# Another recording order for the 586 steps of a fused scan and GELU MLP, with 33 of them on other engines

## The chip, the cores and the metric

The kernel runs on one core of one Trainium2 chip. The metric is the device time in microseconds (us) of one execution; the time of a kernel is the median of its runs. One execution is also recorded by the hardware profiler, and all lines of profiles and traces in this document come from such an execution.

## The reference

A chunked linear recurrence is followed by a two-layer MLP. For each of 4 batches and 8 heads (768 positions, head dimension 32, state size 16):

```python
cum  = np.cumsum(log_a_chunk);  L = exp(cum_i - cum_j) * causal
y    = ((C @ B.T) * L) @ x  +  (C @ state) * exp(cum)          # per chunk
state = exp(sum(log_a_chunk)) * state + sum_j B_j x_j * exp(cum_end - cum_j)
# heads are laid side by side: 3072 tokens x 256
h = tokens @ w_in            # 256 -> 2048
g = gelu_tanh(h)
out = g @ w_out              # 2048 -> 256, 3072 x 256, float32
```

The inputs are float32; the kernel multiplies in bf16 and accumulates in float32.

## The kernel before

**Tiling.** Chunks of 128 positions are used, 6 to a batch, 24 in all. Two chunks make a *unit* u of 256 tokens; there are 12 units, three to a batch. A name such as `s1.3.5` is one step: kind, unit, index.

**The steps of a unit.** `load_x.u` brings x and `castx.u` (L593) casts it to bf16. `G.u` (L599) makes the products of C and B of four head pairs into two PSUM banks ga and gb; `M.u.0` and `M.u.1` (L612, DVE) multiply them by the causal mask. `D.u` (L629) makes the state updates of the two chunks into a bank of the pool hp; `S` (L677) and `SP` (L689), both on DVE, carry the state from chunk to chunk and spread it for the next product. `Y.u` (L642) sums both parts of the output of the scan into the bank yb, and `yev.u` (L673) copies that, as bf16, to where the MLP reads it. Then come eight first products `s1.u.0` to `s1.u.7` (L708: four matmuls of 128x256 into one hp bank), each followed by `gelu.u.i` (L720, ACT), which reads the bank and frees it, and eight second products `s2.c.q` (L725: four matmuls; four q to a chunk c, all into the one bank o, near the end into yb too). `oev.c` (L739) copies the bank o to SBUF, and `store.c` (L744) sends it out. For u from 4 to 11, `G.u` and `D.u` are recorded as a part of `Y.u-1`.

**The steps of a batch.** B and C of a batch are loaded by `load_bc` (L164) and scaled by decay factors: `mul.b.0` (B) and `mul.b.1` (C) (L479). For batch 1 they are turned by TensorE (`T.1.i`, L490, six transposes into ga or gb), copied out (`E.1.i`, L512), C is masked into two halves (`F.1`, L519, two DVE instructions), and B is turned once more (`N.1`, L526, into ga; `bn.1`, L532, copies it out, so that G.3 may write ga again). For batches 2 and 3 a round trip through DRAM does this (`load_wr`, `load_tr`, `load_bn`). The last two chunks of batch 0 have steps of their own of the same kind: `mul1.i` (L442), `T1.i` (L448), `bh1` (L465), `ce1.i` (L458), `N1` (L468), `bn1` (L475). Their factors come from a scan `R` (L375) by the DVE transposes `tp2` (L378, four), `tp6.q` (L385, four) and the reciprocals `recip1` and `recip.1.4` (L382, L389); `pe` and `pp` (L393, L400) make the decay of a whole chunk.

**Weights.** `load_wi.q` and `load_wo.q` bring a quarter of a weight each; `wi.q.k` and `wo.q.k` (L329, L332) cast halves of it to bf16.

**What sets the order.** Every engine runs its instructions in the order in which they were recorded, and the semaphores follow from what reads and writes which tile. The order is a string, `ORDERED` (L17 to L70), of step names; a loop at L945 calls them one after another. `name:A`, `:D` or `:P` moves a step to ACT, DVE or POOL, other than its default. `~n` records n blocks of 128 columns of matmuls on zeros, and `s1.1.3+10` puts ten such blocks ahead of that step; they keep TensorE busy and compute nothing (L705). Buffers that order the work: hp has two banks (each s1, each D), o has one, ga, gb and yb one each, output tiles six.

```python
    for w in ORDERED.split():
        ...
            w, _, n = w.partition("+")
            name, _, e = w.partition(":")
            s = steps[name]
            s.eng, s.pre = e or s.eng, int(n or 0)
            s.fn()
```

Of the kernel before, what the change touches and what calls it, by code (L numbers as in the profile page):

```python
# [19 lines left out]
ew.1.1:A mulc.1 c_bmask c_m8 tw.2 mulb ~4 tw.0 peq ew.0.2:A clip ew.0.1 load_wi.1 ew.0.0:A ew.1.2  # L20
# [6 lines left out]
wo.0.1 T1.0 s1.1.1 T1.1 gelu.1.0 bh1 N1 gelu.1.1 s1.1.2 tp6.0 s1.1.3+10 bn1 ce1.1 load_wo.2
castx.2.None SP.3 wo.0.0 ce1.0 gelu.1.2 gelu.1.3 G.2 s1.1.4 recip.1.4 s1.1.5 gelu.1.4 M.2.1
mul.1.1:P s2.0.0.0.o D.2 M.2.0 load_x.4 gelu.1.5 s2.0.1.0.o s1.1.6 T.1.1 gelu.1.6 S.2.0 s1.1.7
SP.4 Y.2 mul.1.0 yev.2.0.2:D gelu.1.7 wo.1.0 wo.1.1 T.1.0 E.1.1:A castx.3.None:A s1.2.0 wo.2.0  # L30
s1.2.1 E.1.0 wo.2.1 load_wo.3 load_bc.2.1 N.1 gelu.2.0 F.1 s1.2.2 bn.1:D G.3 gelu.2.1 gelu.2.2 D.3
s1.2.3 s2.0.0.1.o S.3.0 S.3.1 load_bc.2.0 gelu.2.3 s1.2.4 M.3.1 s2.0.1.1.o s1.2.5 SP.6 gelu.2.4
s1.2.6 M.3.0 gelu.2.5 wo.3.0:D gelu.2.6 s2.0.0.2.o castx.4.None s1.2.7 Y.3 gelu.2.7 wo.3.1:D
s2.0.1.2.o S.4.0 yev.3.0.2 S.4.1 s2.0.0.3.o oev.0 load_x.5 s1.3.0 s1.3.1 mul.2.1 s2.0.1.3.o
load_wr.2.1 load_x.6 gelu.3.0 gelu.3.1 s1.3.2 oev.1:D SP.8 s1.3.3 s2.1.0.0.o gelu.3.2 M.4.0
gelu.3.3 SP.7 s2.1.0.1.o s2.1.0.2.o s2.1.0.3.o oev.2:D s1.3.4 s1.3.5 s2.1.1.0.o gelu.3.4 M.4.1
mul.2.0:P castx.5.None:A s2.1.1.1.o Y.4 S.5.0 s2.1.1.2.o load_wr.2.0 s2.1.1.3.o load_tr.2.1
load_bn.2 oev.3:D gelu.3.5 s1.3.6 s1.3.7 s2.2.0.0.o yev.4.0.2 load_tr.2.0 gelu.3.6 s1.4.0 SP.9
M.5.1 gelu.3.7 s2.2.0.1.o store.0 store.2 gelu.4.0 s1.4.1 castx.6.None:A s1.4.2 SP.10 s2.2.0.2.o
load_x.7 s2.2.0.3.o gelu.4.1 oev.4:D gelu.4.2 s1.4.3 s1.4.4 load_bc.3.1 s2.2.1.0.o s2.2.1.1.o  # L40
s2.2.1.2.o gelu.4.3 gelu.4.4 s2.2.1.3.o s1.4.5 oev.5 s1.4.6 gelu.4.5 M.5.0 s2.3.0.0.o F.2 store.1
Y.5 s2.3.0.1.o s2.3.0.2.o yev.5.0.2 gelu.4.6 s2.3.0.3.o s1.4.7 S.6.0 gelu.4.7 load_bc.3.0 S.6.1
store.3 s1.5.0 oev.6:D SP.12 s2.3.1.0.o gelu.5.0 s1.5.1 s2.3.1.1.o gelu.5.1 castx.7.None:A
mul.3.1:P s2.3.1.2.o s1.5.2 gelu.5.2 M.6.1 s2.3.1.3.o s1.5.3 M.6.0 Y.6 oev.7:D S.7.0 gelu.5.3
load_x.8 s1.5.4 S.7.1 s2.4.0.0.o s2.4.0.1.o s1.5.5 SP.13 gelu.5.4 load_wr.3.1 yev.6.0.2
castx.8.None store.4 load_x.9 gelu.5.5 SP.14 s2.4.0.2.o s2.4.0.3.o oev.8 s1.5.6 s1.5.7 mul.3.0
castx.9.None s2.4.1.0.o gelu.5.6 load_wr.3.0 gelu.5.7 M.7.0 s2.4.1.1.o s1.6.0 M.7.1 load_tr.3.1
Y.7 S.8.0 load_tr.3.0 gelu.6.0 s1.6.1 s1.6.2 s2.4.1.2.o gelu.6.1 yev.7.0.2:D gelu.6.2 s2.4.1.3.o
oev.9:D M.8.0 s1.6.3 gelu.6.3 SP.16 s1.6.4 s2.5.0.0.o s1.6.5 gelu.6.4 gelu.6.5 M.8.1 SP.15
s2.5.0.1.o s1.6.6 load_bn.3 s2.5.0.2.o s1.6.7 gelu.6.6 s2.5.0.3.o s1.7.0 oev.10:D gelu.6.7 s1.7.1  # L50
gelu.7.0 s2.5.1.0.o s1.7.2 store.5 gelu.7.1 s2.5.1.1.o gelu.7.2 s1.7.3 gelu.7.3 s1.7.4 gelu.7.4
store.9 F.3 s2.5.1.2.o s1.7.5 s1.7.6 gelu.7.5 s2.5.1.3.o s1.7.7 gelu.7.6 store.6 Y.8 oev.11
yev.8.0.2:D gelu.7.7 S.9.0 load_x.10 s2.6.0.0.o s2.6.0.1.o s2.6.0.2.o S.9.1 s1.8.0 gelu.8.0
s2.6.0.3.o s1.8.1 gelu.8.1 oev.12:D s1.8.2 gelu.8.2 s2.6.1.0.o castx.10.None:D store.10 store.11
store.7 s1.8.3 gelu.8.3 s2.6.1.1.o s1.8.4 gelu.8.4 s1.8.5 s2.6.1.2.o s2.6.1.3.o SP.18 M.9.1
gelu.8.5 s1.8.6 M.9.0 store.8 oev.13 gelu.8.6 Y.9 store.12 s2.7.0.0.o s2.7.0.1.o S.10.0 s2.7.0.2.o
yev.9.0.2:D s2.7.0.3.o S.10.1 s1.8.7 oev.14 s1.9.0 load_x.11 castx.11.None:A gelu.8.7 M.10.0
s2.7.1.0.o s2.7.1.1.o SP.21 s1.9.1 s2.7.1.2.o s2.7.1.3.o gelu.9.0 SP.20 gelu.9.1 oev.15 s1.9.2
M.10.1 SP.19 gelu.9.2 Y.10 s1.9.3 gelu.9.3 store.15 S.11.0 s1.9.4 M.11.0 s2.8.0.0.o s1.9.5
gelu.9.4 store.14 s2.8.0.1.o gelu.9.5 s2.8.0.2.o SP.22 s2.8.0.3.o s1.9.6 store.13 gelu.9.6  # L60
oev.16:D s1.9.7 gelu.9.7 yev.10.0.2:D s2.8.1.0.o s1.10.0 s2.8.1.1.o s1.10.1 gelu.10.0 s1.10.2
s2.8.1.2.o gelu.10.1 s1.10.3 s2.8.1.3.o M.11.1 oev.17:D gelu.10.2 s1.10.4 store.17 gelu.10.3
s1.10.5 Y.11 yev.11.0.2:D gelu.10.4 s2.9.0.0.o s1.10.6 gelu.10.5 s2.10.0.0.yb s2.9.0.1.o
s2.10.0.1.yb s1.10.7 s2.10.0.2.yb s2.9.0.2.o gelu.10.6 s2.9.0.3.o s1.11.0 gelu.10.7 s1.11.1 oev.18
s2.9.1.0.o gelu.11.0 store.16 s2.10.0.3.yb s1.11.2 s2.9.1.1.o oev.20 gelu.11.1 s2.9.1.2.o
gelu.11.2 s1.11.3 s2.9.1.3.o gelu.11.3 oev.19:D s1.11.4 s1.11.5 s2.11.0.0.yb gelu.11.4 s1.11.6
gelu.11.5 s2.10.1.0.o store.20 s1.11.7 gelu.11.6 s2.11.0.1.yb s2.10.1.1.o s2.10.1.2.o store.19
s2.10.1.3.o gelu.11.7 oev.21:D s2.11.0.2.yb s2.11.0.3.yb s2.11.1.0.o oev.22:D s2.11.1.1.o store.22
# [915 lines left out]
```

## Time and profile before

| | us |
|---|---|
| median of 3 runs (118.0, 118.29, 121.6) | 118.29 |
| span of the profiled execution, first to last instruction | 116.9 |
| what lies around the span, against the median | 1.4 |
| TensorE matmuls busy in the span | 110.1 |
| DVE busy | 69.4 |
| ACT busy | 72.1 |
| POOL busy | 21.4 |

The profile gives no time of the profiled execution other than its span. A line of the timeline has the start, the time from the first start to the last end, engine, source line, operation, tiles, shapes and count; in square brackets stands how long the engine was idle before it and what it waited for. `PE` is TensorE, `SPq` the DMA queue that SyncE issues to. Where a line has a count over 1 its instructions follow each other.

### The profile page before, as it was taken

To read this page: it belongs to the slowest core of one execution; us is meant where nothing else is said; L and a number is where in the kernel's file an instruction comes from. 1 tells how busy PE (TensorE), PEld (TensorE's weight loads), DVE (VectorE), ACT (ScalarE), POOL (GpSimd) and SP (SyncE) were. 2 spreads that over 40 slices of the span, in tenths; PEclk is the share of its full clock that TensorE was granted. 3 is DMA by queue.
4 is the path that set the end of the run, shared out by engine and by line. 5 is a ranking of instruction groups with operands and counts; after the bars stand their busy time and mean duration, and the time that the engine had idled before them with its cause. 6 is when DMAs were issued, how large, how long until landed. Compare 5 with 4: busy or idle time off the path is not lost.

```text
span 116.9 us, 3379 instructions
## 1 busy us (share of the span) xinstructions
PE 110.1 (94%) x1426; PEld 92.0 (79%) x1426; DVE 69.4 (59%) x140; ACT 72.1 (62%) x139; POOL 21.4 (18%) x38
## 2 busy tenths in 40 slices
...
PEclk9999999999999999999999999999999999999999
...
GB/s 26 228 332 357 281 252 178 208 288 257 305 143 90 185 47 219 213 253 200 72 25 171 121 163 63 0 140 98 40 6 63 71 0 52 43 0 50 45 47 132
DMA packets 43007, 15.97 MB, mean 137 GB/s; under 512 B 36657, under 2 KB 41457, under 8 KB 42993
## 3 DMA queue, kind: packets, MB, share of 16 engines
...
q8 instruction: 11, 0.18, 0.6%
q10 hardware_dynamic: 192, 0.13, 0.5%
...
HBM read 11.04 MB, written 3.93 MB: 128 GB/s over the span
## 4 chain that ended last, share of the span: by engine, by line
PE 75%; DMA 8%; DVE 6%; SPq 6%; issue 2%; POOL 1%; ACT 0%; DVEq 0%; POOLq 0%
PE o_ps L735 33%; PE hp L717 30%; DMA bcf<-in_B_dram 8%; PE yb L735 3%; SPq L190 3%; PE ga L603 3%; PE yb L658 2%; DVE m L613 2%; PE yb L667 2%; DVE ce L523 1%; SPq L150 1%; DVE bh L327 1%; DVE bc L484 1%; SPq L159 1%; SPq L183 1%
## 5 line engine op out<-in xcount | busy, mean ns | idle before, releaser
L721 ACT ACTIVATE gT<-hp 128x512 bf16<-128x512 f32 x96 | 54.3, 596 | 25.0 <-PE hp L717 24.6
L717 PE MATMUL hp<-xm,w_in_sb 128*128 128x256 bf16 x384 | 53.3, 273 | 0.6 <-ACT gT L721 0.4
L735 PE MATMUL o_ps<-w_out_sb,gT 128*128 128x256 bf16 x352 | 47.3, 273 | 0.0
L717 PEld LDWEIGHTS <-w_in_sb 128*128 128x128 bf16 x384 | 41.4, 114 | 3.5 <-issue 1.9
L735 PEld LDWEIGHTS <-gT 128*128 128x128 bf16 x384 | 37.0, 98 | 4.9 <-issue 1.1
L327 DVE COPY o_sb<-o_ps 128x256 f32<-128x256 f32 x13 | 5.5, 425 | 23.8 <-PE o_ps L735 20.4
L613 DVE TENSOR_TENSOR m<-ga,tri 128x1024 bf16<-128x1024 f32 x12 | 14.6, 1218 | 0.1
L613 DVE TENSOR_TENSOR m<-gb,tri 128x1024 bf16<-128x1024 f32 x11 | 13.4, 1219 | 0.7 <-PE gb L603 0.7
L323 ACT ACTIVATE o_sb<-o_ps 128x256 f32<-128x256 f32 x9 | 3.5, 385 | 9.2 <-PE o_ps L735 9.2
L705 PE MATMUL yb<-wz 128*128 128x512 bf16 (+3 forms) x23 | 7.6, 481 | 1.1 <-DVE wz L220 1.1
L691 DVE SCALAR_TENSOR_TENSOR sp_new<-s_new,pend,bmask 128x256 bf16<-128x256 f32 x17 | 7.9, 476 | 0.0
L327 DVE CAST xm<-yb 128x512 bf16<-128x512 f32 x6 | 4.1, 687 | 5.8 <-PE hp L636 4.8
L684 DVE SCALAR_TENSOR_TENSOR s_new<-s_new,pend,hp 128x64 f32<-128x64 f32 x13 | 3.6, 279 | 6.4 <-PE hp L636 6.2
L705 PEld LDWEIGHTS <-wz 128*128 128x128 bf16 x26 | 3.0, 120 | 5.1 <-issue 3.2
L667 PE MATMUL yb<-m,x 128*32 128x128 bf16 x192 | 6.1, 220 | 0.0
L603 PE MATMUL ga<-ce,bh 32*128 32x256 bf16 x48 | 4.7, 273 | 1.3 <-DVE bn L327 0.9
L484 POOL TENSOR_TENSOR bc<-bc_t,pt 128x768 bf16<-128x768 f32 x2 | 3.0, 1494 | 13.8 <-DMA bc_t<-in_C_dram 13.7
L658 PE MATMUL yb<-ce,sp_new 128*32 128x128 bf16 x160 | 5.3, 221 | 0.0
L603 PE MATMUL gb<-ce,bh 32*128 32x256 bf16 x48 | 4.7, 273 | 0.0
L735 PE MATMUL yb<-w_out_sb,gT 128*128 128x256 bf16 x32 | 4.6, 273 | 0.0
L667 PEld LDWEIGHTS <-x 128*32 128x32 bf16 x192 | 3.8, 97 | 0.8 <-issue 0.8
L323 ACT ACTIVATE xm<-yb 128x512 bf16<-128x512 f32 x6 | 3.6, 595 | 1.1 <-PE hp L636 1.1
...
## 6 DMA issues: line engine op xcount, KB each, us to landing
...
```

Source lines behind the costliest of these rows:

```text
L323: nc.scalar.activation(o, i, AF.Copy)
L327: nc.vector.tensor_copy(out=o, in_=i)
L484: (nc.gpsimd if eng == "POOL" else nc.vector).tensor_tensor(out=d["bc16"][:, i], in0=d["bc"].rearrange("p i h (r n) -> p i r h n", r=R6)[: ...
L603: nc.tensor.matmul(out=gbank(g)[:, 256 * k:256 * k + 256], lhsT=bh_of(2 * u + k)[gs], rhs=ce_of(2 * u + k)[gs], start=True, stop=True, til ...
L613: nc.vector.tensor_tensor(out=m_of(u)[:, 2 * i:2 * i + 2].rearrange("p g k e t -> p (g k e) t"), in0=gx[i].rearrange("p g (k t) -> p (g k) ...
L658: nc.tensor.matmul(out=y4[32 * j:32 * j + 32, k, w], lhsT=sp[:, 32 * h:32 * h + 32], rhs=ce_of(gc)[:, h % 2], start=first(j), stop=False, ...
L667: nc.tensor.matmul(out=y4[32 * j:32 * j + 32, k, w], lhsT=X16[u][:, k, 32 * h:32 * h + 32], rhs=m[:, h // 2, h % 2, :], start=first(j), st ...
L691: nc.vector.scalar_tensor_tensor(out=sp_new.rearrange("p (g d) -> p g d", g=4), in0=(XN[0][:, H * D:H * D + 64] if gc == 0 else state[("s" ...
L705: nc.tensor.matmul(out=t[:, 0:m * 128], lhsT=wz, rhs=w3.to_broadcast([128, m, 128]), start=True, stop=True, skip_group_check=True)
L717: nc.tensor.matmul(out=hp[:, j * T:(j + 1) * T], lhsT=w_in_k[:, w, q, k], rhs=xm[:, w, u * T:(u + 1) * T], start=(w == 0), stop=(w == 1))
L721: nc.scalar.activation(gts[u][:, 2 * i:2 * i + 2], hps.pop((u, i)).rearrange("p (j t) -> p j t", j=2), AF.Gelu_apprx_tanh)
L735: nc.tensor.matmul(out=ops[gc], lhsT=gts[u][:, fi, k * Q:(k + 1) * Q], rhs=w_out_sb[:, fi, :], start=(fi == 0 and (u > 0 or k == 0)), stop ...
```

## The change

Only the string `ORDERED` is changed. It names the same 586 steps. As the recorded instruction lists of the two kernels stand:

- Up to `s1.0.0` every engine's order is the same; `c_wz` is written ahead of the loads, but it is the first DVE instruction in both.
- All DMAs on SyncE's queue stand in the same order, loads, round trips and stores.
- After `s1.0.0`, TensorE, DVE, ACT and POOL each have another order.
- The ten blocks of zeros at `s1.1.3` are gone.
- 33 steps change engine: to DVE `ce1.0`, `ce1.1`, `E.1.1`, `mul.1.1`, `wo.1.1`, `castx.6`, `oev` 0, 8, 11, 13, 15; to POOL `wi.3.0`, `mul.1.0`, `castx.3`, `wo.3.0`, `mul.2.1`, `castx.5`, `castx.11`; to ACT `yev` 2, 7, 8, 9, 10, 11, `bn.1`, `wo.2.1`, `wo.3.1`, `castx.10`, `oev` 2, 6, 7, 12, 22. Among them `mul.1.0` and `mul.1.1` swap DVE and POOL.

The stretch in question, by engine, up to G.3:

```
before PE:   s1.0.0 G.1 s1.0.1..6 Y.1 pp s1.0.7 s1.1.0 T1.0 s1.1.1 T1.1 N1 s1.1.2 (10 blocks) s1.1.3 G.2 s1.1.4 s1.1.5
             s2.0.0.0 D.2 s2.0.1.0 s1.1.6 T.1.1 s1.1.7 Y.2 T.1.0 s1.2.0 s1.2.1 N.1 s1.2.2 G.3 D.3
after PE:    s1.0.0 G.1 s1.0.1..6 Y.1 pp T1.0 T1.1 s1.0.7 N1 s1.1.0 s1.1.1 G.2 D.2 s1.1.2 s1.1.3 s2.0.0.0 s1.1.4 s2.0.1.0
             s1.1.5 s1.1.6 Y.2 T.1.0 s1.1.7 s1.2.0 T.1.1 N.1 s1.2.1 s1.2.2 s2.0.0.1 s2.0.1.1 D.3 G.3
before DVE:  SP.1 M.1.1 M.1.0 wi.3.0 SP.2 pe tp6.2 tp2 tp6.3 recip1 S.1.1 tp6.1 tp6.0 SP.3 recip.1.4 M.2.1 M.2.0 S.2.0
             SP.4 mul.1.0 yev.2 E.1.0 F.1 bn.1
after DVE:   tp2 recip1 M.1.0 SP.1 SP.2 M.1.1 pe tp6.0 S.1.1 tp6.2 tp6.3 tp6.1 ce1.1 ce1.0 recip.1.4 S.2.0 M.2.1 M.2.0
             SP.4 SP.3 mul.1.1 E.1.0 wo.1.1 E.1.1 F.1
before POOL: ... wi.3.1 mul1.0 mul1.1 wo.0.1 castx.2 wo.0.0 mul.1.1 wo.1.0 wo.1.1 wo.2.0 wo.2.1 castx.4 mul.2.0 mul.3.1
after POOL:  ... wi.3.1 wi.3.0 mul1.1 mul1.0 wo.0.1 castx.2 wo.0.0 mul.1.0 castx.3 wo.1.0 wo.2.0 wo.3.0 castx.4 mul.2.1 castx.5 mul.2.0 mul.3.1
```

The diff, cut to its first lines; the rest of the string is changed in the same manner:

```diff
-load_aq.0 load_aq.1 load_aq.2 load_aq.3 c_wz load_bc0.1 c_ident c_m4 c_sel c_tri c_zero load_bc0.0
+c_wz load_aq.0 load_aq.1 load_aq.2 load_aq.3 load_bc0.1 c_ident c_m4 c_sel c_tri c_zero load_bc0.0
...
-load_wi.3 S.1.0 s1.0.0 SP.1 xn.2 load_bc1.1 wi.2.0 gelu.0.0 G.1 s1.0.1 s1.0.2 M.1.1 M.1.0
-load_bc1.0 load_wo.0 wi.3.0:D gelu.0.1 wi.2.1 s1.0.3 load_x.2 SP.2 pe wi.3.1 gelu.0.2 load_bc.1.1
+S.1.0 s1.0.0 xn.2 tp2 gelu.0.0 G.1 wi.2.0 s1.0.1 xn.3 recip1 M.1.0 s1.0.2 wi.2.1 gelu.0.1 s1.0.3
+load_bc1.1 SP.1 SP.2 M.1.1 pe tp6.0 gelu.0.2 s1.0.4 wi.3.1 wi.3.0 S.1.1 tp6.2 mul1.1:P gelu.0.3
...
```

From Y.3 on, both orders weave s1 of a later unit with s2 of an earlier one. The new one starts the second products of a unit earlier: `s2.1.0.0` follows Y.3 at once, where before seven steps of s2 and s1 of other chunks stood between.

More of the change, by code (lines that the diff above doesn't have):

```diff
@@ L17 @@
 ORDERED = """
[L18 removed]
+c_wz load_aq.0 load_aq.1 load_aq.2 load_aq.3 load_bc0.1 c_ident c_m4 c_sel c_tri c_zero load_bc0.0
 c_unp load_a.0:A clipq load_x4 Rq tpq recip0 c_cz mulc.0 ~59 tw.1 load_wi.0 c_warm load_a.1:A
[L20 removed]
+ew.1.1:A mulc.1 c_bmask c_m8 tw.2 mulb ~4 tw.0 peq ew.0.2 clip ew.0.1 load_wi.1 ew.0.0:A ew.1.2
@@ L27 @@
[L27 to L68, printed above, removed]
```

49 lines of the change are left out of this document (45 added, 4 removed).

## The prediction

> **What bounds the kernel now.** I read the page first, then the busy time by stretch, then the waits of TensorE with its timeline, and last the timelines of the engines that it waited for. The page:
>
> ```profile
> span 116.9 us, 3379 instructions
> PE 110.1 (94%) x1426; PEld 92.0 (79%) x1426; DVE 69.4 (59%) x140; ACT 72.1 (62%) x139; POOL 21.4 (18%) x38
> ...
> PEclk9999999999999999999999999999999999999999
> ```
>
> TensorE is busy for 94% of the span, at the full granted clock. Where the other 6% lies is told by three stretches, cut at the first s1 (12.50), at G.3 (29.69) and at the end of TensorE's work (columns: length, then busy time and instructions of each engine):
>
> ```profile
> 12.50:29.69 17.19, 15.34 (x197) 11.66 (x198) 15.99 (x30) 14.58 (x30) 9.55 (x15) 1.00 1.04 239
> 29.69:113.90 84.21, 84.18 (x1080) 75.25 (x1079) 43.43 (x76) 50.61 (x94) 5.01 (x5) 1.00 0.44 100
> 113.90:116.90 3.00, 0.00 (x0) 0.00 (x0) 0.00 (x0) 0.38 (x1) 0.00 (x0) 1.00 0.39 132
> ```
>
> From 29.69 on TensorE is busy 84.18 of 84.21 us: only TensorE work counts there, an order can lose but not win. The start (12.5) and the tail (3.0) hold the same steps in both kernels. What can be won lies between 12.50 and 29.69, where DVE is busy 15.99 of 17.19 us. TensorE's rows there:
>
> ```profile
> 16.96 0.29 PE L658 MATMUL yb<-ce,sp_new 128*32 128x128 bf16 x8
> 19.22 0.28 PE L452 MATMUL ga<-ident,bc0s 128*128 128x128 bf16 x2 [0.24 <-POOL bc0s L444]
> 25.46 0.29 PE L658 MATMUL yb<-ce,sp_new 128*32 128x128 bf16 x8
> 29.69 0.28 PE L603 MATMUL ga<-ce,bh 32*128 32x256 bf16 x2 [0.89 <-DVE bn L327]
> 30.02 0.24 PE L636 MATMUL hp<-x,bn 128*32 128x64 bf16 x8
> 30.20 0.63 PE L717 MATMUL hp<-xm,w_in_sb 128*128 128x256 bf16 x4
> 37.91 1.75 PE o_ps L735 x16
> ```
>
> They are Y.1, T1.0, Y.2, G.3, D.3, the first dense s1, and (from the chain of waits) four s2 steps in 1.75, so 0.437 a step, s1 and s2 alike. G.3 waited for DVE's bn.1; before it stand 19 s1 and 2 s2. So G.3 marks the end of a stage that DVE sets, and what it is worth is: when it starts, and how many steps TensorE has behind it by then.
>
> DVE's rows of that stage, two weight casts, and one F step from later:
>
> ```profile
> 12.83 0.48 DVE L691 SCALAR_TENSOR_TENSOR sp_new<-s_new,pendq,bmask 128x256 bf16<-128x256 f32 x1
> 13.48 1.23 DVE L613 TENSOR_TENSOR m<-gb,tri 128x1024 bf16<-128x1024 f32 x1 [0.17 <-PE gb L603]
> 14.62 1.22 DVE L613 TENSOR_TENSOR m<-ga,tri 128x1024 bf16<-128x1024 f32 x1
> 15.75 0.42 DVE L327 CAST w_in_sb<-wf 128x512 bf16<-128x512 f32 x1
> 16.93 1.94 DVE L351 STREAM_TRANSPOSE rt<-r_t 32x192 f32<-32x192 f32 x6
> 18.90 0.25 DVE L383 RECIPROCAL pt<-rt 128x16 f32<-128x16 f32 x1
> 19.29 1.07 DVE L351 STREAM_TRANSPOSE rt<-r_t 32x192 f32<-32x192 f32 x2
> 22.24 1.23 DVE L613 TENSOR_TENSOR m<-gb,tri 128x1024 bf16<-128x1024 f32 x1 [0.55 <-PE gb L603]
> 24.82 0.48 DVE L691 SCALAR_TENSOR_TENSOR sp_new<-s_new,pend,bmask 128x256 bf16<-128x256 f32 x1
> 25.22 0.95 DVE L484 TENSOR_TENSOR bc<-bc_t,rt 128x768 bf16<-128x768 f32 x1
> 26.14 0.69 DVE L327 CAST xm<-yb 128x512 bf16<-128x512 f32 x1
> 26.78 0.96 DVE L327 COPY bh<-ga 128x768 bf16<-128x768 bf16 x1
> 27.65 1.52 DVE L523 TENSOR_SCALAR ce<-ch,par 128x768 bf16<-128x768 bf16 x2
> 29.09 0.54 DVE L327 COPY bn<-ga 128x768 bf16<-128x768 bf16 x1
> 33.44 0.76 DVE L327 CAST w_out_sb<-wf 128x512 bf16<-128x512 f32 x2
> 48.73 0.74 DVE L523 TENSOR_SCALAR ce<-ch,par 128x768 bf16<-128x768 bf16 x2
> ```
>
> DVE's instructions start before the last one's end is drawn, so prices go from start to start: M 1.14, SP 0.40. One row stands out: F.1 (27.65) took 1.52, F.2 (48.73), the same two instructions, 0.74. POOL tells why:
>
> ```profile
> 18.54 0.62 POOL L444 TENSOR_TENSOR bc0s<-bcf,rt 128x256 bf16<-128x256 f32 x1 [3.59 <-DVE rt L351]
> 21.88 1.49 POOL L484 TENSOR_TENSOR bc<-bc_t,pt 128x768 bf16<-128x768 f32 x1
> 27.67 1.29 POOL L325 CAST w_out_sb<-wf 128x512 bf16<-128x512 f32 x2 [0.23 <-DMA wf<-in_moe_w_out_dram]
> 35.28 2.01 POOL L484 TENSOR_TENSOR bc<-bc_t,rt 128x768 bf16<-128x768 f32 x1 [5.31 <-DMA bc_t<-in_B_dram]
> ```
>
> Two weight casts ran on POOL from 27.67 to 28.96, and F.1 ended 0.21 after them: 0.78 of F.1 is standing still beside POOL. The other way round, the POOL product at 35.28 took 2.01 instead of 1.49; a DVE product of the same form was running then. That decides the forecast.
>
> **The change part by part.** *DVE up to G.3.* In before DVE needs from 12.83 to the release of G.3, 29.63 (29.09 + 0.54). Taken from this list: wi.3.0 to POOL (0.38, half of the 33.44 row), yev.2 to ACT (26.78 - 26.14 = 0.64), bn.1 to ACT (0.54), F.1's standing still (1.52 - 0.74 = 0.78, since in the new order only one weight cast can still meet it), and the two waits for G (0.17 + 0.55), since tp2 and recip1 now fill the first and six steps of DVE lie between G.2's inputs and M.2.1. Sum 3.06. Added: ce1.1 and ce1.0 (256 columns from PSUM: a third of E.1.0's 0.96 at the least, the 0.42 of 15.75's 512 columns at the most; I keep 0.41 each, 0.82), E.1.1 (0.87, 26.78 to 27.65), wo.1.1 (0.38), and about 0.30 of waiting for T.1.0 ahead of E.1.0, as Y.2, T.1.0 and E.1.0 now follow each other with nothing between. Sum 2.37. mul.1.1 for mul.1.0 is an even trade, and the transposes only change place. Without anything else G.3 is released at 29.63 - 3.06 + 2.37 = 28.94.
>
> *POOL beside DVE.* This is what speaks against it. wi.3.0 comes on POOL right when SP.1 and SP.2 now run: SP.1 is due at 12.83 + 0.97 (four tp2: the six transposes at 16.93 to 18.90 less two of 0.50) + 0.17 (recip1, 18.90 to 19.07 by its successor) + 1.14 (M.1.0) = 15.11. POOL then has wi.3.0 and mul1.1, 0.62 each. If each SP stands still as F.1 did, that is 0.25 + 0.35. Then mul.1.0 on POOL: its input landed at 17.84 + 5.5 = 23.35:
>
> ```profile
> L168 SPq DMA_DIRECT2D bc_t<-in_B_dram x1: 582/582/582, 17.8 to 17.8; - x1
> DMA to landing us min/median/max: 5.5/5.5/5.5
> ```
>
> so it runs from 23.4 to 24.9, and DVE comes to SP.4 at about 24.5: SP.4 waits, SP.3 waits for castx.3 behind it, 0.4 in all. wo.1.1 meets wo.2.0 on POOL, 0.2. Sum 1.2, and G.3 is released at 28.94 + 1.2 = 30.15. The rows show both a DVE instruction with one input and a POOL product held up; an SP or a product on DVE behind POOL isn't shown. By the Trainium skill, "SBUF — State Buffer", section "Who interferes with whom", the shared port pair is an exclusive lock: a DVE instruction with two SBUF inputs and a GpSimd one that reads SBUF exclude each other, whichever started first. The rows at 27.65 and 35.28 agree; by that rule the 1.2 are paid, and going only by what the rows show directly just wo.1.1's 0.2 would be sure.
>
> *TensorE by then.* In the new order 19 s1, 4 s2 and D.3 stand before G.3: two s2 (0.87) and D.3 (30.20 - 30.02 = 0.18) more, 1.05 in all. Summed step by step TensorE itself is ready for G.3 at about 30.1 in the slow case (Y.2 at 25.75, then 0.56, T.1.0 0.34, two s1, T.1.1 and N.1 0.34 each, two s1, two s2, D.3, some waiting at N.1), at 29.2 in the fast one. So G.3 at 30.15 with 1.05 more done: 1.05 - (30.15 - 29.69) = 0.6 won.
>
> *The zeros.* The ten blocks lie before G.2, in a stretch that waits for DVE: nothing by themselves (at most 0.54, ten blocks of 128 columns at 2.4 columns a ns by the 0.437 for 1024). If DVE were no longer the bound they would count in full.
>
> *T1 ahead of s1.0.7.* TensorE now needs mul1.0 at about 18.0 instead of 19.22. Its input is on the chain of waits:
>
> ```profile
> 7.75 8.91 DMA bcf<-in_B_dram
> ```
>
> It lands at 16.66; with 0.62 on POOL it is done at 17.3. Hidden with 0.7 left; later it would move T1, N1 and G.2.
>
> *ACT.* It takes yev.2, bn.1 (bound below by 0.54, above by the 0.96 of E.1.0), wo.2.1 and wo.3.1, and gives up E.1.1, ce1 and castx.3. In the stretch it was busy 14.58 of 17.19 and G.3 has two s2 in front of it: hidden.
>
> *From G.3 on.* 77 s1 and 92 s2 remain. I looked at each copy of bank o: two s1 (0.87) always stand between the last s2 of a chunk and the first of the next, as before, and a copy takes 0.43 and some 0.2 for its two hand-overs:
>
> ```profile
> L327 DVE COPY o_sb<-o_ps 128x256 f32<-128x256 f32 x13 | 5.5, 425 | 23.8 <-PE o_ps L735 20.4
> ```
>
> The closest masks are M.10.1 before Y.10 and M.11.0 before Y.11: nine steps (3.93) of TensorE against 3.3 of DVE (two M, two SP, a copy), 0.6 left. Nothing paid. If such a cover fails, it costs up to its own 0.4 each time.
>
> *DMAs.* The queue's order is unchanged. mul.2.1 now goes through POOL before castx.5 and mul.2.0, so load_wr.2.0 is issued about 1.1 later; Y.5 needs what comes of it at about 52.7 by the same summing of steps, and
>
> ```profile
> 42.90 1.23 SPq L505 DMA_TRANSPOSE bh<-scr x1
> ```
>
> the last transfer was issued at 42.90: hidden.
>
> *Sum.* 0.6 off the span: 116.9 gives 116.3; with the 1.4 around it, off the median of 118.29, 117.7. The tail after 113.91 is the same.
>
> **The rivals.** *DVE isn't held up by POOL in SP and mul.1.1.* For it: no row shows that. Then DVE releases G.3 at 28.94 and TensorE, ready at 29.2, is the bound: 1.05 + 29.69 - 29.2 = 1.5 won, 116.8. *The standing still is worse:* mul.1.0 takes 2.01 (35.28 row), and SP.4 to mul.1.1 alternate with it and castx.3: 0.5 to 0.6 more, all of the gain; 118.3. *Slower: a late landing now hurts.* In before mul.1.0 runs at 25.22, 1.9 after its input's landing; now T.1.0 waits on POOL, the earliest 1.5 after the landing, and E.1.0, E.1.1, F.1 and G.3 hang behind it. With Y.2 at 25.75 and 0.56 for it, T.1.0 can bear a landing up to 24.8; from 25.4 on the gain is gone and each us costs one. The bcf load took 8.9 to land; the same here gives 26.75, 1.35 beyond that: 119.7. Against it: that load was issued with four weights ahead of it, and the order of the queue is the same. *The order does not do what it says:* the recorded lists agree up to s1.0.0 on every engine, so only the mean over runs could differ.
>
> **How the numbers follow.** Held up by POOL as in F.1: 0.43, 117.7 (117.2 to 118.2 by 0.5 more or less of standing still). Not held up: 0.25, 116.8, down to 116.4 if the waits ahead of Y.2 go too. All lost: 0.14, 118.3. Late landing: 0.12, 119.7. The rest, 0.06, is a cover from G.3 on that fails often, or DVE's stage becoming free altogether. The range 116.4 to 119.2 leaves out the late landing's upper part and the rest. Two per cent, 115.9 and 120.7, are about what a measurement of this kernel can tell from no change; none of the main cases crosses them: faster 0.05, within 0.86, slower 0.09 (a landing later still, or failing covers).
>
> **What would show it.** G.3's start (L602 now) against 30.15, with four s2 before it; F.1's two instructions near 0.8 in sum; SP.4 or SP.3 lengthened from 0.48 while a POOL product runs, or not; T.1.0 waiting for DVE or PE, not for POOL; no wait of TensorE after G.3. It is wrong if TensorE waits on bank o, on ga/gb, or on a DMA after G.3, or if the granted clock leaves 1.00.

## The result, and the profile after

The forecast was 117.7 us (116.4 to 119.2). The changed kernel took 119.17 us (median of 10 executions, 118.45 to 120.09) beside 118.35 for the kernel before, a ratio of 1.0066 with a 95% interval of 1.0038 to 1.0094: slower by a little, where a gain of 0.6 us was forecast. That 119.17 still lies inside the range, by 0.03, is luck: the upper part of the range stood for a late landing that holds up T.1.0, and no profile shows T.1.0 waiting for POOL. A ratio leaves out executions more than 1.5% above the fastest of the same kernel, which in one experiment below (sp_ahead) is five of twelve, so medians and groups are given beside it.

The page of the profile after, and its three stretches, cut as in the prediction at the first s1, at G.3 and at the end of TensorE's work:

```profile
span 117.3 us, 3376 instructions
PE 109.7 (94%) x1423; PEld 92.0 (78%) x1423; DVE 66.8 (57%) x133; ACT 74.1 (63%) x142; POOL 23.7 (20%) x42
```

```profile
13.05:30.69 17.64, 15.48 (x210) 12.35 (x211) 16.95 (x31) 13.80 (x28) 8.45 (x13) 1.00 1.04 238
30.69:113.80 83.11, 83.10 (x1072) 74.39 (x1064) 39.17 (x68) 53.15 (x99) 8.37 (x9) 1.00 0.44 97
113.80:117.28 3.48, 0.00 (x0) 0.00 (x0) 0.00 (x0) 0.38 (x1) 0.00 (x0) 0.85 0.34 113
```

In this execution the middle stretch is as forecast almost to the digit: 17.64 from the first s1 to G.3 (forecast 17.65), 83.11 behind it instead of 84.21 (1.10 more work done by then, forecast 1.05), no waiting behind G.3. What differs is the start, 13.05, and the end, 3.48 instead of 3.00. The rows of DVE and POOL ahead of G.3, TensorE's waits, and its rows of Y.2 and G.3 say how the 17.64 came about:

```profile
25.08 1.04 DVE L690 SCALAR_TENSOR_TENSOR sp_new<-s_new,pend,bmask 128x256 bf16<-128x256 f32 x2
26.05 1.36 DVE L483 TENSOR_TENSOR bc<-bc_t,pt 128x768 bf16<-128x768 f32 x1
29.57 0.75 DVE L522 TENSOR_SCALAR ce<-ch,par 128x768 bf16<-128x768 bf16 x2
```

```profile
22.45 1.50 POOL L483 TENSOR_TENSOR bc<-bc_t,rt 128x768 bf16<-128x768 f32 x1 [2.33 <-DMA bc_t<-in_B_dram]
24.84 0.61 POOL L324 CAST x<-x_t 128x512 bf16<-128x512 f32 x1 [0.88 <-DMA x_t<-in_x_dram]
```

```profile
PE ga L602 <- DVE ce L462: 0.7, 1, 0.7
PE yb L657 <- DVE sp_new L690: 0.4, 1, 0.4
PE hp L401 <- DVE pe L395: 0.3, 1, 0.3
```

```profile
26.18 0.29 PE L657 MATMUL yb<-ce,sp_new 128*32 128x128 bf16 x8 [0.44 <-DVE sp_new L690]
30.69 0.28 PE L602 MATMUL ga<-ce,bh 32*128 32x256 bf16 x2
```

F.1 took 0.75, as forecast. mul.1.0 ran on POOL from 22.45 to 23.95, and SP.4 came to DVE only at 25.08: in this execution the two did not meet, and the pair of SPs took 1.04, close to the 0.87 that it takes alone (pool_free below). The 0.17 between goes with castx.3, on POOL from 24.84 to 25.45. So the 17.64 agrees with the forecast in part by chance, since the 0.4 that the forecast had for this pair was not paid.

G.3 itself waits for nothing. From Y.2 on, which waited for SP.3, TensorE runs through to G.3 in 4.51. In the kernel before G.3 waited for DVE; in this order what counts is when DVE is done with SP.3, and a DVE step behind that (mul.1.1, wo.1.1, F.1) can be longer without moving G.3.

### The profile page after: what moved, and what is told of

It reads as the page before. It is cut to its first block, busy times and chain, and to the rows that moved or that the text cites. A ratio compares the mean times of both kernels' runs of the same rounds, so it can differ in the third digit from the quotient of the medians.

```text
span 117.3 us, 3376 instructions
## 1 busy us (share of the span) xinstructions
PE 109.7 (94%) x1423; PEld 92.0 (78%) x1423; DVE 66.8 (57%) x133; ACT 74.1 (63%) x142; POOL 23.7 (20%) x42
## 4 chain that ended last, share of the span: by engine, by line
PE 81%; DVE 12%; ACT 2%; issue 2%; DVEq 0%
PE o_ps L734 32%; PE hp L716 31%; PE yb L704 5%; DVE m L612 4%; PE yb L734 3%; DVE rt L350 3%; PE ga L602 2%; PE yb L657 2%; DVE sp_new L690 2%; PE yb L666 2%; ACT ce L322 1%; DVE s_new L683 1%; DVE ce L462 1%; DVE pt L390 1%; PE o_ps L570 1%
## 5 line engine op out<-in xcount | busy, mean ns | idle before, releaser
L734 PE MATMUL o_ps<-w_out_sb,gT 128*128 128x256 bf16 x352 | 46.8, 273 | 0.0
L326 DVE COPY o_sb<-o_ps 128x256 f32<-128x256 f32 x14 | 5.9, 424 | 24.3 <-PE o_ps L734 23.8
L324 POOL CAST x<-x_t 128x512 bf16<-128x512 f32 x7 | 4.3, 614 | 29.0 <-DMA x_t<-in_x_dram 29.0
L704 PE MATMUL yb<-wz 128*128 128x512 bf16 (+3 forms) x23 | 8.3, 512 | 1.1 <-DVE wz L219 1.1
L322 ACT ACTIVATE xm<-yb 128x512 bf16<-128x512 f32 x12 | 7.2, 596 | 1.0 <-PE yb L666 0.8
L681 DVE COPY s_new<-hp 128x64 f32<-128x64 f32 x3 | 0.7, 226 | 7.4 <-PE hp L635 7.4
```

Of the source, the lines that this page charges most:

```text
L322: nc.scalar.activation(o, i, AF.Copy)
L326: nc.vector.tensor_copy(out=o, in_=i)
L704: nc.tensor.matmul(out=t[:, 0:m * 128], lhsT=wz, rhs=w3.to_broadcast([128, m, 128]), start=True, stop=True, skip_group_check=True)
L734: nc.tensor.matmul(out=ops[gc], lhsT=gts[u][:, fi, k * Q:(k + 1) * Q], rhs=w_out_sb[:, fi, :], start=(fi == 0 and (u > 0 or k == 0)), stop ...
```

## Experiments

Unless something else is said, a run has the changed kernel's order with the edit shown. Each diff is of the order string; a line of "..." stands for words in between.

**The same two kernels again** (no edit).

> The kernel before, unchanged, to see how far its start, its stage up to G.3 and its close repeat. In the first two profiles s1.0.0 started at 12.50 (before) and 13.05 (changed), though both orders agree up to there, and the close after the last copy took 2.99 and 3.48. If both are chance of one execution, this profile can show the late start or the long close too, and the median stays at 118.35. If they belong to the changed order, it shows 12.5 and 3.0 again.

> The changed kernel, unchanged. Chance theory: s1.0.0 anywhere from 12.5 to 13.1, close 3.0 or 3.5, G.3 17.6 after s1.0.0. Order theory: s1.0.0 at 13.05 and close 3.48 again. Median 119.2 in both.

Measured: 118.40 (ratio 1.0008, 0.9979 to 1.0037) and 118.83 (1.0059, 1.0029 to 1.009). So the loss is real: 0.82 and 0.44 us by the medians, 0.78 and 0.70 by the ratios. But the profiles of the same kernels are not the same. Before, by stretch and F.1; after, by stretch, then POOL and DVE around SP.4, and TensorE's rows of Y.2 and G.3:

```profile
12.17:28.80 16.63, 15.34 (x197) 11.65 (x198) 15.42 (x30) 14.35 (x30) 8.78 (x14) 1.00 0.98 229
28.80:113.00 84.20, 84.17 (x1080) 75.26 (x1079) 43.71 (x76) 50.95 (x95) 5.34 (x6) 1.00 0.46 104
```

```profile
27.34 0.95 DVE L523 TENSOR_SCALAR ce<-ch,par 128x768 bf16<-128x768 bf16 x2
```

```profile
12.08:30.95 18.87, 15.62 (x210) 12.28 (x210) 17.70 (x31) 14.07 (x29) 10.45 (x14) 1.00 0.98 239
30.95:114.06 83.11, 83.10 (x1072) 74.40 (x1064) 38.90 (x68) 53.16 (x99) 8.32 (x9) 1.00 0.43 98
```

```profile
23.90 1.49 POOL L483 TENSOR_TENSOR bc<-bc_t,rt 128x768 bf16<-128x768 f32 x1 [3.21 <-DMA bc_t<-in_B_dram]
...
24.28 1.39 DVE L690 SCALAR_TENSOR_TENSOR sp_new<-s_new,pend,bmask 128x256 bf16<-128x256 f32 x1
...
25.33 0.81 POOL L324 CAST x<-x_t 128x512 bf16<-128x512 f32 x1
```

```profile
26.48 0.29 PE L657 MATMUL yb<-ce,sp_new 128*32 128x128 bf16 x8 [1.54 <-DVE sp_new L690]
30.96 0.28 PE L602 MATMUL ga<-ce,bh 32*128 32x256 bf16 x2
```

The stretch up to G.3 took 16.63 where the prediction's profile had 17.19 (F.1 stood still 0.2 instead of 0.78), and 18.87 where the first profile after had 17.64. Behind G.3 both kernels repeat to 0.01. In the second profile after, mul.1.0 began on POOL at 23.90; SP.4, on DVE from 24.28, ended 0.28 after it (24.28 + 1.39 = 25.67 against 25.39) instead of after its own 0.48, SP.3 then stood behind castx.3, and TensorE waited 1.5 for them. From Y.2 to G.3 it took 4.48, again without a wait. Of the two theories each is right on one point: the start is chance (12.08 in the changed kernel), the longer end belongs to the order (3.50 again, 3.02 in before_again). That the stretch up to G.3 would be 1.2 us longer neither of them foresaw.

**Half of the change.** early_new has the changed order up to Y.3 and the words of the kernel before behind it; late_new the other way round (with the s1 and GELUs of unit 3 moved so that two s1 stand by each copy of bank o).

```diff
 (early_new, from Y.3 on)
-yev.3.0.2 oev.0:D oev.1:D s2.1.0.0.o s2.1.0.1.o S.4.0 S.4.1
+load_bc.2.1 load_bc.2.0 S.4.0 yev.3.0.2 S.4.1 oev.0 load_x.5
...
 (late_new, from the kernel before, from Y.3 on)
-gelu.2.7 wo.3.1:D s2.0.1.2.o S.4.0 yev.3.0.2 S.4.1 s2.0.0.3.o oev.0
+wo.3.1:A gelu.2.7 yev.3.0.2 s2.0.1.2.o s2.0.0.3.o s2.0.1.3.o oev.0:D oev.1:D
...
```

> The new order up to Y.3, the remaining steps in the old order with the old engines. If the early part costs the time (POOL and DVE in each other's way, a start that depends on when loads land), about 119.1. If the early part wins the 0.6 that was forecast and the late part loses it again, about 117.7.

> The old order up to Y.3, the remaining steps in the new order with the new engines; s1 and gelu of unit 3 are put so that each copy of bank o still has two s1 beside it. If the early part costs the time, about 118.3. If the late part does, 119.2 or more.

Measured: 119.59 (1.013, 1.0081 to 1.018) and 119.27 (1.0098, 1.0062 to 1.0135). Each half is slower than either whole, so the sum of the halves says nothing; joining two orders makes waits that neither has (late_new: 0.7 for a GELU behind G.3; early_new: 0.6 in all behind G.3). Read by the time alone, early_new (119.1 expected if the early part costs) and late_new (119.2 or more if the late part does) would each put the whole loss into its own half. The rows still tell something. The stretch up to G.3 was 18.64 in early_new and 17.16 in late_new, so the new order is the longer one here too. early_new showed the largest standing still so far:

```profile
24.68 1.49 POOL L483 TENSOR_TENSOR bc<-bc_t,rt 128x768 bf16<-128x768 f32 x1 [3.10 <-DMA bc_t<-in_B_dram]
24.76 1.69 DVE L690 SCALAR_TENSOR_TENSOR sp_new<-s_new,pend,bmask 128x256 bf16<-128x256 f32 x1
```

and the longer end went with the late half: 3.00 in early_new, 3.49 in late_new.

**Is it POOL beside SP.4 and SP.3?** Two ways to take the meeting away.

```diff
 (sp_ahead)
-M.2.1 M.2.0 SP.4 gelu.1.2 SP.3 gelu.1.3
+SP.4 SP.3 M.2.1 M.2.0 gelu.1.2 gelu.1.3
 (pool_free)
-mul.1.0:P
+mul.1.0
...
-castx.3.None
+castx.3.None:A
```

> The changed kernel with one edit: SP.4 and SP.3 (the two expansions of the state, two SBUF inputs) stand ahead of the two masks M.2.1 and M.2.0 on VectorE instead of behind them; the same instructions on the same engines. Theory A (SP.4 and SP.3 stand still because GpSimd's mul.1.0 and castx.3 run beside them; the masks read PSUM and do not, 1.22 us in every run whether GpSimd runs or not): SP.4 and SP.3 start at about 22.0 to 22.8, before most of mul.1.0 (22.45 to 24.68 in the runs so far), and take 0.8 to 1.5 us together instead of 1.04, 2.14 and 2.44; TensorE's wait for sp_new (0.4, 1.5, 1.8) is gone; the masks end up to 0.8 later; the stage from s1.0.0 to G.3 falls from 17.64 to 18.87 to about 17.3 to 17.8, the time by 0.3 to 0.8 us to about 118.0 to 118.5. Rival B (the sum over VectorE sets G.3, wherever the work stands): SP.4 and SP.3 as long as before, or mul.1.1 and others lengthened in their place; stage 17.6 to 18.9, time 118.8 to 119.2.

> The changed kernel with mul.1.0 on VectorE (right behind mul.1.1) and castx.3 on ScalarE, so that GpSimd does nothing beside SP.4 and SP.3. Theory A: SP.4 and SP.3 take 0.85 us together (0.48 each alone), instead of 1.04 to 2.44; VectorE gets 0.95 more for mul.1.0, ScalarE 0.7 for castx.3. T.1.0 then waits for mul.1.0 on VectorE, ends about 24.3 + 0.85 + 0.95 + 0.95 = 27.1 plus, against 27.3 to 28.4 now: G.3 at about the same to 0.8 earlier, time 118.3 to 119.0. Rival B (no standing still; the lengths come from something else on VectorE): SP.4 and SP.3 stay at 2 us together and the added 0.95 is paid: 119.7 or more.

sp_ahead: 118.72 (0.9989, 0.9943 to 1.0034). Its executions fall into two groups of six, 117.63 to 118.42 and 119.01 to 119.83. The profile is of the lower group; DVE, then POOL:

```profile
22.05 0.88 DVE L690 SCALAR_TENSOR_TENSOR sp_new<-s_new,pend,bmask 128x256 bf16<-128x256 f32 x2
22.85 1.22 DVE L612 TENSOR_TENSOR m<-gb,tri 128x1024 bf16<-128x1024 f32 x1
23.98 1.22 DVE L612 TENSOR_TENSOR m<-ga,tri 128x1024 bf16<-128x1024 f32 x1
```

```profile
23.86 1.49 POOL L483 TENSOR_TENSOR bc<-bc_t,rt 128x768 bf16<-128x768 f32 x1 [3.50 <-DMA bc_t<-in_B_dram]
```

The same start of mul.1.0 as in the second profile after (23.86, 23.90), but the SPs take 0.88 instead of 2.14, and the mask beside mul.1.0, which has one of its inputs in PSUM, takes its 1.22. The stretch is 17.55 instead of 18.87: 1.3 us for two words moved. Theory A holds in the profile; the median, with its upper group, does not follow it, and is 0.39 above that of the kernel before.

pool_free: 119.35 (1.0089, 1.0056 to 1.0121), slower than expected. DVE, and a wait of TensorE:

```profile
24.51 0.87 DVE L690 SCALAR_TENSOR_TENSOR sp_new<-s_new,pend,bmask 128x256 bf16<-128x256 f32 x2
25.30 0.95 DVE L483 TENSOR_TENSOR bc<-bc_t,pt 128x768 bf16<-128x768 f32 x1
26.17 0.95 DVE L483 TENSOR_TENSOR bc<-bc_t,rt 128x768 bf16<-128x768 f32 x1
```

```profile
PE ga L492 <- DVE bc L483: 1.1, 1, 1.1
```

The SPs take 0.87, as theory A says; rival B (the length comes from something else on DVE) falls. But B's product is now third in DVE's line and T.1.0 waits 1.1 for it: one stall was exchanged for another, the stretch is 18.64.

**The end of the program.** castx.11 is POOL's last step in the changed kernel (at 79 us); the kernel before has it on ACT and its last POOL step at about 57 us.

```diff
 (close_a, from after)
-castx.11.None
+castx.11.None:A
 (close_b, from before)
-castx.11.None:A
+castx.11.None
```

> The changed kernel with castx.11 on ScalarE, as in the kernel before, instead of on GpSimd: GpSimd's last step is then castx.9. Theory A (the close, from the last matmul's start to the end of the span, is 0.47 us longer because GpSimd's last working instruction is castx.11 at 79 us): the close falls from 3.78 to 3.30, the time by about 0.4 us to 118.4 to 118.7. Rival B (it is the number of instructions in GpSimd's program, or the order of stores, that lengthens it): the close stays at 3.77 to 3.79, time 118.8 to 119.2. ScalarE gets 0.7 us at 79 us, where TensorE never waited for it: no cost.

> The kernel before with castx.11 on GpSimd instead of on ScalarE: the mirror of the run before. Theory A (GpSimd's late last step lengthens the close): the close rises from 3.30 to 3.78, the time from 118.4 to about 118.8. Rival B (length of GpSimd's program or the order of stores): 3.30, or a value between if each instruction counts; time 118.3 to 118.5.

Measured: 118.59 (1.0021, 0.9984 to 1.0057) and 118.52 (1.0016, 0.9985 to 1.0048), too near to their parents for the time alone to decide. The last stretch, from TensorE's end to the end of the span, of close_a, then of close_b:

```profile
113.45:116.80 3.35, 0.00 (x0) 0.00 (x0) 0.00 (x0) 0.38 (x1) 0.00 (x0) 0.81 0.35 117
```

```profile
113.43:116.45 3.02, 0.00 (x0) 0.00 (x0) 0.00 (x0) 0.38 (x1) 0.00 (x0) 1.00 0.39 132
```

Within the span neither did what theory A expected (3.30 and 3.78 by that text's cut, which begins 0.30 earlier; 3.65 and 3.31 came). But the span is not the whole time. For each execution the time less the span is known too, and it is steady:

| kernel | castx.11 on | end in the span | time less span, median | together |
|---|---|---|---|---|
| before | ACT | 3.00 | 1.95 (1.78 to 2.08) | 4.95 |
| early_new | ACT | 3.00 | 1.97 (1.89 to 2.00) | 4.97 |
| close_a | ACT | 3.35 | 1.73 (1.67 to 1.78) | 5.08 |
| pool_free | POOL | 3.01 | 2.19 (2.14 to 2.25) | 5.20 |
| close_b | POOL | 3.02 | 2.19 (2.14 to 2.25) | 5.21 |
| after, after_again | POOL | 3.48, 3.50 | 1.70 (1.66 to 1.78) | 5.19 |
| late_new | POOL | 3.49 | 1.73 (1.70 to 1.78) | 5.22 |

Together they sort by castx.11's engine, and the runs below fit: about 5.1 in the four with close_a's edit, about 5.2 in the others. close_b, one word away from before, pays 0.26; close_a gives back 0.11 of after's 0.24, and what the other 0.13 goes with is open. Why a POOL step 34 to 38 us before the end (82.9 in close_b, 79.5 in after) costs that, these runs don't show.

**When B lands.** In the kernel before, POOL multiplies C and DVE multiplies B; in the changed kernel the two have changed engines, and C is still loaded first. So POOL, the slower engine for it, waits for the table that lands second. b_first exchanges the two loads; fix_sp puts the two earlier edits together; fix_sp_ce moves half of ce1 back to ACT as well.

```diff
 (b_first)
-load_bc.1.1 G.2 D.2 gelu.1.1 S.2.0 load_bc.1.0
+load_bc.1.0 G.2 D.2 gelu.1.1 S.2.0 load_bc.1.1
 (fix_sp: the edits of sp_ahead and close_a; fix_sp_ce: these and)
-ce1.0:D
+ce1.0
```

> The changed kernel with one edit: the loads of batch 1's B and C tables change places, so that the table that GpSimd multiplies (B, mul.1.0) lands first, as the table that GpSimd takes does in the kernel before. Theory A (the landing of B sets when mul.1.0 runs on GpSimd, and with it whether SP.4 and SP.3 stand still): mul.1.0 starts on GpSimd at 20.5 to 22.0 instead of 22.45 to 24.68 and ends before SP.4 starts at about 24.3 to 25.1; SP.4 and SP.3 take 0.85 to 1.1 us together instead of 1.04 to 2.44; the stage from s1.0.0 to G.3 is 17.4 to 17.7 and the time 0.3 to 0.9 below the changed kernel's, 118.1 to 118.6. Rival B (other work on GpSimd, castx.3 and the casts of w_out, does it, or the landing is not set by the order of the two loads): SP.4 and SP.3 stay at 1.3 to 2.4, the time at 118.8 to 119.2. A third way: C now lands last, at 22.4 to 24.7, and VectorE's mul.1.1 waits for it at 25; then the wait moves to C and nothing is won.

> The changed kernel with two edits that each did something alone: SP.4 and SP.3 ahead of the masks M.2.1 and M.2.0, and castx.11 on ScalarE. Theory A (the two add up: up to 1.3 us in the stage up to G.3 where B lands late, 0.1 to 0.25 at the end): SP.4 and SP.3 0.88 together, stage 17.5 to 17.7; last matmul's start at 112.2 to 112.8, the last matmul to the end of the measured time 5.25 to 5.4 instead of 5.5; time 117.8 to 118.3, with some executions 1.3 higher as in the run with the first edit alone if what sets those two groups has nothing to do with castx.11. Rival B (the first edit's gain in the profile is not there in the median): 118.5 to 118.8.

> The run before with one more edit: one of the two parts of ce1 (ce1.0) back on ScalarE, where the kernel before has both. The changed kernel has them on VectorE, 0.88 us for the two, and TensorE waits 0.7 for the second at G.2 in every profile. Theory A (VectorE's order up to M.2.0 sets Y.2 and then G.3): the reciprocal, S.2.0 and all behind start 0.4 earlier, TensorE's wait at G.2 shrinks from 0.7 to 0.3 or less, G.3 0.2 to 0.4 earlier, time 0.2 to 0.4 below the run before. Rival B (ScalarE, between bh1 and the GELUs, is late with ce1.0, or B's landing is next in line): no gain, or up to 0.5 more.

b_first: 118.81 (1.0024, 0.9999 to 1.0049). DVE; POOL; TensorE:

```profile
24.31 0.87 DVE L690 SCALAR_TENSOR_TENSOR sp_new<-s_new,pend,bmask 128x256 bf16<-128x256 f32 x2
```

```profile
21.40 1.50 POOL L483 TENSOR_TENSOR bc<-bc_t,rt 128x768 bf16<-128x768 f32 x1 [0.62 <-DMA bc_t<-in_B_dram]
...
33.30 0.61 POOL L324 CAST w_out_sb<-wf 128x512 bf16<-128x512 f32 x1 [4.12 <-DMA wf<-in_moe_w_out_dram]
```

```profile
33.97 1.03 PE L734 MATMUL o_ps<-w_out_sb,gT 128*128 128x256 bf16 x8 [1.05 <-POOL w_out_sb L324]
```

mul.1.0 at 21.40, the SPs 0.87, the stretch 17.38, the shortest of this order: theory A again. Of the 1.5 us that the stretch gains on the second profile after, 1.05 are given back 4 us later, where TensorE waits for the cast of the last quarter of w_out. Two things meet there: G.3 is early (29.76), and the quarter landed late, so that its cast began at 33.30, where it had begun at 30.92 and 31.15 in the two profiles after. fix_sp shows the same (cast at 32.97, wait 0.57; 118.83, 1.0036, 1.0008 to 1.0065). In sp_ahead, with G.3 at 29.62 and the cast at 31.25, there was no such wait. fix_sp_ce missed: 120.77 (1.0189, 1.0151 to 1.0227). On ACT, ce1.0 waits for the part that DVE still does, and the GELUs queue behind it:

```profile
21.55 0.47 ACT L460 ACTIVATE ce<-gb,par 128x256 bf16<-128x256 bf16 x1 [1.68 <-DVE ce L462]
```

```profile
PE hp L716 <- ACT gT L720: 2.6, 4, 1.9
```

**The next load in line.** The last quarter of w_out one place earlier, alone and with the edits before.

```diff
 (wo3; sp_wo3: with sp_ahead's edit; sp_wo3_close: with close_a's too)
-load_x.4 bn.1 s1.2.2 s2.0.0.1.o gelu.2.1 F.1 load_wo.3
+load_wo.3 load_x.4 bn.1 s1.2.2 s2.0.0.1.o gelu.2.1 F.1
```

> The changed kernel with one edit: the load of the last quarter of w_out is issued ahead of that of x.4 instead of behind it. Theory A (a second loss of the changed order lies behind G.3: the changed kernel wants that quarter at about 33.5 to 34, two s1 blocks sooner than the kernel before, and it lands at 30.8 to 33.3 by the execution; but as long as SP.4 and SP.3 stand still, G.3 is so late that it is there): the quarter lands about 1 us earlier, no execution waits for it, and the median falls by 0 to 0.3 us only, 118.6 to 119.0, with fewer executions above 119.3. Rival B (it is not the landing): nothing moves, 118.8 to 119.2; or x.4, now later, is waited for by castx.4 and S.4: 0.3 to 0.8 more.

> The changed kernel with both edits: SP.4 and SP.3 ahead of the masks, and the load of w_out's last quarter ahead of x.4's. Theory A: the first edit alone brought G.3 0.1 to 1.3 us forward and made two groups of executions (six at 117.6 to 118.4, six at 119.0 to 119.8), since w_out's last quarter then decides in some of them (waits of 0.6 and 1.05 us for its cast in two such profiles); with the load earlier the upper group goes, the stage is 17.4 to 17.7, no wait for the w_out cast, median 117.9 to 118.4. Rival B (the two groups come from something else, say the start): two groups as before, median 118.6 to 118.8.

> The run before with castx.11 on ScalarE in addition. Theory A: the last matmul to the end of the measured time falls from 5.5 to 5.38, so 0.1 to 0.2 below the run before: 117.8 to 118.3, below the kernel before by 0.1 to 0.5. Rival B: castx.11's engine does not matter to the time; same as the run before.

wo3: 119.09 (1.0069, 1.0043 to 1.0095): alone it does nothing; in its profile the SPs still took 2.10, and G.3 is late anyway (stretch 18.44). sp_wo3: 118.64 (1.003, 0.9997 to 1.0063), sp_wo3_close: 118.55 (1.0017, 0.9979 to 1.0056). The wait for w_out is gone in both, and there are still two groups (sp_wo3: seven at 118.12 to 118.66, five at 119.19 to 119.60), so theory A of these runs falls: w_out does not make the groups. This time the profile is of the upper group, and shows what is likely to:

```profile
22.37 1.50 POOL L483 TENSOR_TENSOR bc<-bc_t,rt 128x768 bf16<-128x768 f32 x1 [2.26 <-DMA bc_t<-in_B_dram]
22.51 1.63 DVE L690 SCALAR_TENSOR_TENSOR sp_new<-s_new,pend,bmask 128x256 bf16<-128x256 f32 x1
```

B landed early here, so that POOL was at its product just when the SPs, now ahead of the masks, came. SP.4 ended at 24.14, 0.27 after POOL, and the pair took 2.03. sp_wo3_close's profile, of the upper group too, agrees (mul.1.0 from 22.12, the pair 1.60); in sp_ahead's, of the lower group, they were 23.86 and 0.88. Three profiles make this likely, not shown. Where mul.1.0 has C's load ahead of it, it began at 22.12, 22.37, 22.45, 23.01, 23.70, 23.86, 23.90, 23.97, 24.48 and 24.68 in ten profiles. Behind the masks (24.3 to 25.1) the SPs meet the late landings, ahead of them (22.0 to 22.7) the early ones. By these rows sp_ahead did not take the meeting away, it chose other executions for it.

**The meeting with mul.1.0 taken away at every landing.** B first, and w_out's last quarter one place earlier; DVE's and POOL's orders are the changed kernel's.

```diff
 (b_wo3: the edits of b_first and wo3; b_wo3_close: with close_a's too)
-load_bc.1.1 G.2 D.2 gelu.1.1 S.2.0 load_bc.1.0
+load_bc.1.0 G.2 D.2 gelu.1.1 S.2.0 load_bc.1.1
...
-load_x.4 bn.1 s1.2.2 s2.0.0.1.o gelu.2.1 F.1 load_wo.3
+load_wo.3 load_x.4 bn.1 s1.2.2 s2.0.0.1.o gelu.2.1 F.1
```

> The changed kernel with two edits of the order of the loads only: B of batch 1 ahead of C, and w_out's last quarter ahead of x.4. VectorE's order is the changed kernel's. What the runs so far say: with B first GpSimd's mul.1.0 starts at 21.4 instead of 22.1 to 24.7 and is over before SP.4 starts at 24.3, whenever in that range B lands, so SP.4 and SP.3 should take 0.87 in every execution; and the w_out load, which cost 1.05 us of waiting in the run with B first alone, lands 1.5 to 2 us sooner. Theory A: stage 17.3 to 17.6, no wait for the w_out cast, executions in one group, median 118.1 to 118.4, the same as the kernel before within its interval or a little below. Rival B (something further is next in line: C's landing for mul.1.1, castx.3 beside mul.1.1, x.4): 118.6 to 118.9.

> The run before with castx.11 on ScalarE in addition, which took 0.1 to 0.2 off the end of the program. Theory A: 117.9 to 118.3, 0.1 to 0.5 below the kernel before. Rival B: the engine of castx.11 does not matter, 118.1 to 118.4 as the run before; or the next stall in line shows, 118.6 to 118.9.

Measured: 118.46 (1.0001, 0.9973 to 1.0028) and 118.39 (0.9994, 0.9965 to 1.0024), b_wo3's twelve executions in one group, 117.68 to 119.06. b_wo3, by stretch, then POOL, and the SPs:

```profile
12.60:30.51 17.91, 15.49 (x210) 12.35 (x211) 16.73 (x31) 13.98 (x29) 10.32 (x15) 1.00 0.99 234
30.51:113.62 83.11, 83.10 (x1072) 74.39 (x1064) 38.91 (x68) 53.12 (x99) 7.55 (x9) 1.00 0.43 99
```

```profile
21.24 1.49 POOL L483 TENSOR_TENSOR bc<-bc_t,rt 128x768 bf16<-128x768 f32 x1 [0.58 <-DMA bc_t<-in_B_dram]
24.69 0.61 POOL L324 CAST x<-x_t 128x512 bf16<-128x512 f32 x1 [1.96 <-DMA x_t<-in_x_dram]
```

```profile
24.93 1.04 DVE L690 SCALAR_TENSOR_TENSOR sp_new<-s_new,pend,bmask 128x256 bf16<-128x256 f32 x2
```

With B first mul.1.0 began at 21.40, 21.24 and 21.48 in three profiles, and was over before SP.4 each time. The pair took 1.04, and 1.13 in b_wo3_close, not the 0.87 that was expected "in every execution": castx.3 still lies beside it. The stretch was 17.91 and 18.05, also more than the 17.3 to 17.6 expected, though both profiles are of executions slower than their median (118.86 and 118.91). So theory A's time came, and the stretch that should have given it is not in the two profiles.

Exchanging two pairs of loads, and moving nothing that computes, brings the changed kernel level with the kernel before. No version beats the kernel before by more than its interval.

## Why the prediction was wrong, point by point

A sum over profiles with the same order up to G.3 (before: the first, before_again, close_b; after: the first, after_again, close_a), in us:

| term | before | after | difference | forecast |
|---|---|---|---|---|
| first s1 | 12.50, 12.17, 12.46 | 13.05, 12.08, 12.27 | +0.09 | 0 |
| first s1 to G.3 | 17.19, 16.63, 16.78 | 17.64, 18.87, 18.06 | +1.32 | +0.46 |
| G.3 to TensorE's end | 84.21 | 83.11 | -1.10 | -1.05 |
| end, with the time outside the span | 4.95 | 5.19 | +0.24 | 0 |
| sum | | | +0.55 | -0.6 |

Measured: +0.82 and +0.44 by the medians. Three profiles of each are a small sample of a stretch that spreads by 1.2; late_new (17.16) and early_new (18.64), with the same two orders up to Y.3, would make the difference 1.36.

The step that failed is **POOL beside DVE**, "SP.4 waits, SP.3 waits for castx.3 behind it, 0.4 in all", and with it the 1.2 of the whole term. The mechanism was right and named; its size was taken from one landing, 23.35, which in the changed kernel is one draw from 22.1 to 24.7. Up to Y.2, where it counts, DVE stood still beside POOL for this long:

| | first profile after | after_again | close_a | forecast |
|---|---|---|---|---|
| SP.1 and SP.2 | 0.45 | 0.78 | 0.46 | 0.6 |
| pe | 0.35 | 0 | 0.38 | 0 |
| SP.4 and SP.3, against 0.87 alone | 0.17 | 1.27 | 0.39 | 0.4 |
| sum | 0.97 | 2.05 | 1.23 | 1.0 |

Only in after_again was it mul.1.0 that the last pair met; in the other two it was castx.3 alone. On the mean this is 0.4 more than forecast, and so the largest of three errors, not the whole: the stretch of the kernel before was forecast 0.3 too long, and the end 0.24 too short. DVE's rows of SP.1 and SP.2 (0.87 alone) and of pe (0.14 alone) in the first profile after:

```profile
15.59 1.32 DVE L690 SCALAR_TENSOR_TENSOR sp_new<-s_new,pendq,bmask 128x256 bf16<-128x256 f32 x2
...
17.97 0.49 DVE L393 TENSOR_TENSOR pe<-ac,r_t 64x3 f32<-64x3 f32 x1
```

Step by step:

- *The first stretch's 17.19* was one draw too: F.1's 0.78 of standing still, which I let the change remove, was 0.2 in before_again. Three profiles average 16.87, so 0.3 of the forecast gain was never there. The "1.4 around the span" hid this: the time less the span is 1.95 in this kernel, so the profiled 116.9 belongs to an execution of about 118.85, not to the median.
- *The other terms of DVE up to G.3* hold: ce1 0.88 (forecast 0.82), the wait ahead of M.2.1 gone, F.1 0.75.
- *The rest of POOL beside DVE*: wo.1.1 lost 0.05 in the first profile after and 0.35 in close_a (forecast 0.2), and mul.1.1 took 1.36 instead of 0.95 in the first. These lie behind SP.3, and Y.2 to G.3 took 4.51, 4.48 and 4.48 all the same: they cost nothing, and the forecast's 0.2 for wo.1.1 was not paid.
- *TensorE by then*: right (1.10 for 1.05). The forecast had DVE and TensorE reach G.3 within 0.1 of each other; in the three profiles it was TensorE that came last, from Y.2 on.
- *From G.3 on nothing paid*: right for the changed kernel as it is (83.10 busy of 83.11, twice), but one cover was missing from my list: the w_out quarter, needed sooner now, is late where G.3 is early and the quarter lands late.
- *Zeros, ACT, T1*: hidden, as forecast; no row shows TensorE waiting for bc0s or for bank o. (1024 columns in 0.437 are 2.34 a ns, not 2.4: 0.55 for the zeros.)
- *The tail holds the same steps*: wrong by 0.24. A step that moves to POOL at 79 us was costed as DVE, ACT and POOL time, and lies beside other work; its price is at the end. close_b shows it, close_a only half of it.
- *Rivals.* "Standing still is worse" (0.14, 118.3) was the nearest in mechanism and size; it should have been the forecast's upper half, not a rival, since nothing held mul.1.0 to 23.4. "A late landing now hurts" had the landing right, 23.9 to 24.7 came often, but the wrong victim: T.1.0 bore it as worked out (up to 24.8), the SPs did not. "Not held up" falls.

By the Trainium skill, "SBUF — State Buffer", section "Who interferes with whom", a DVE instruction with two SBUF inputs and a GpSimd one that reads SBUF contend for a shared port pair, and whichever comes first holds it for its whole instruction. The traces agree: an SP that began behind mul.1.0 ended 0.27 to 0.28 after it at three different starts (by 24.28 + 1.39 = 25.67 for 25.39, 24.76 + 1.69 = 26.45 for 26.17, and 22.51 + 1.63 = 24.14 for 23.87 in the rows above), never after half of it. F.1, which the prediction counted as agreeing, has one large SBUF input: that it stands still too is shown by its row alone.
